# Transforms copied out of PSUM once, folds and sums from SBUF, and a new list order

## The chip, the cores and the metric

The kernel runs on one core of one Trainium2 chip. The metric is device microseconds of one execution, the median over runs. The kernel before took 450.99 us: three runs of 451.47, 450.99 and 449.7.

## The reference, cut to what matters

```python
x = A_x                                        # 2048 x 448, float32
xn = layernorm(x)                              # mean and variance over 448
y = irfft2(rfft2(xn) * (w_r + 1j * w_i))       # over both axes
gate, up = x @ W_gate, x @ W_up                # 448 -> 1792
h = gate * (gate > 0) * up
return x + y + h @ W_down                      # 1792 -> 448
```

Two branches stand side by side: a Fourier filter over the whole of the normalised input, and a gated feed-forward layer. Everything is float32. TensorE is given float16 high and low parts (three products for one) where that is enough.

## The kernel before, in words

**Feed-forward branch.** The 1792 features are 14 tiles of 128, in three groups of 5, 5 and 4. The 2048 tokens are four chunks of 512, taken in the order 0, 2, 1, 3. One feature tile of one chunk is a gate unit, 56 in all: 28 matmuls of 128x512 into one of two PSUM buffers named `gu`. A gate step follows each unit: ScalarE applies the ReLU (L1058), VectorE multiplies by the up half (L1062), ScalarE makes the float16 high part `h` (L1066), VectorE the low part (L1070). When a group's units of one chunk are done, down units (`dn`, 128x448) follow: ScalarE seeds the accumulator (L1087) and takes it out again (L1098). At the very end `dn_end` does the last four token tiles without a seed; its last 12 matmuls (L1126) go into the transforms' buffer.

**Forward transform.** Tokens are split as 16 columns of 128 rows of work; columns a and a+8 are a pair, and the eight pairs are taken in the order 0, 4, 2, 6, 1, 5, 3, 7. For one pair:

- `f_dft`: 48 small matmuls (`fx<-fd_t,T`), the transform along the 448.
- `f_dft` ends with a ScalarE copy of one half of the result (L527); `f_fold` (L539, twice) adds and subtracts the other half, read from PSUM, to give `eb`.
- `f_a` and `f_b`: an eight-point butterfly on `eb` on VectorE (L463 to L468, L473 to L490).
- `f_sdft`: four float32 matmuls (`fx<-eb,fm`, eight rows of the trace) along the tokens.
- `f_y1`: one half copied by ScalarE (L611), then sum and difference with the other half, read from PSUM (L615, L616).

The butterflies across pairs (`stage2` to `stage4`, L590 to L604), the product with the filter and the inverse butterflies follow.

**Inverse transform**, for one pair p: `i_pair` joins two sides, `i_mix` does the eight-point butterfly on `wst` (half 0 is L463 to L468, half 1 is L477 to L490), `i_hi` and `i_lo` make the float16 parts `vt` (L840, L845), `i_sdft` is 48 matmuls (`fx<-im,vt`), `i_part` copies one half of the result (L864), `i_unfold` adds and subtracts the other half from PSUM (L869, twice), `i_pqhi` and `i_pqlo` make the float16 parts `wf` (L875, L879), and `i_ddft` is 48 matmuls (`fx<-idc_t,wf`). `i_ddft` is seeded and taken out by ScalarE (L890, L906), and the rows are stored.

All transforms share one PSUM buffer of two banks, `fx`: a transform can begin only when all readers of the one before it are done. `two_banks` opens it for `f_dft` with a ScalarE write of one element (L507).

**What sets the order.** The opening (loads, layer norm, weights, the first gate units) stands in an order written out by hand (`OPENING`). From there the program issues gate and down units in a fixed sequence, and between them items of one list, `bg`. Each item has a cost in VectorE microseconds:

```python
add(1.27, f_fold, 0)                       # cost, function, arguments
```

Each gate or down unit earns credit, and `run_bg` issues list items while the credit lasts. So the list's order and costs decide behind which TensorE unit a step is issued. Two list entries are special: `offer` lets a transform be placed inside the next unit, between two half-height passes that stand together (`gu_halves`), and `force` places it now if that has not happened. The framework's scheduler then sets each engine's final order by priority; `tc.high_priority` pulls matmuls of a block together and the copies forward. All engines run their own queue in order.

Of the kernel before, what the change touches and what calls it, by code (L numbers as in the profile page):

```python
# [19 lines left out]
KC = 29  # L20
# [142 lines left out]
def tile_gfnet_reglu(ctx: ExitStack, tc: tile.TileContext, x, xr, wgu, wd, wf, ident, c_fd, c_fm, c_im, c_row, c_id,  # L163
# [289 lines left out]
        copy(Tq[q][:, (3, 4, 8)[i], :], tp["end", i], act)  # L453


    fi = {}
    Fq, Xh, yps, cur, fa, fps = {}, {}, {}, {}, {}, {}
    RT = float(np.sqrt(0.5))

    def eight_a(F, w):  # L460
# [48 lines left out]

    def f_dft(a, b, m=None):  # L510

        ps = fps[a] = two_banks()
        T = Tq[a % 4]
        for k, n2 in enumerate((a, b)):
            js = slice(128 * (n2 // 4), 128 * (n2 // 4 + 1))
            for r in range(4):
                o = slice((4 * k + r) * GW, (4 * k + r + 1) * GW)
                for i, (t, part) in enumerate(((r, "h"), (r, "l"), (5 + r, "h"))):
                    c = fd_off[part, r]
                    for h in (1, 0):  # L520
                        p = slice(64 * h, 64 * h + 64)
                        with tc.high_priority(offset=2000):
                            m = chained(mm(ps[:, 1 - h, o], T[p, t, js], fd_t[p, c:c + GW], start=(k + r + i == 0),
                                                 stop=(i == 2), skip_group_check=True).ins, m)
        t = fa[a] = free.pop(0)
        with tc.high_priority(offset=400):
            A.activation(flat(t).rearrange("p (i e) -> p i e", i=2), ps[:, :, 0:4 * GW], AF.Copy,  # L527
                         scale=2.0 ** -14)
        return m

    def f_fold(a):

        k = fi[a] = NG * (len(fi) % 2)
        F = Fq[a] = state["eb"][:, k:k + NG]
        F = F.rearrange("p (i s) c (b k) -> p b i (s c) k", i=2, b=2)
        t = flat(fa[a]).rearrange("p (i x k) -> p i x k", i=2, k=KC)
        ps = fps.pop(a)[:, :, 4 * GW:8 * GW].rearrange("p i (x k) -> p i x k", k=KC)
        for b in range(2):
            V.scalar_tensor_tensor(F[:, b], ps, (-1.0) ** b * 2.0 ** -14, t, op0=OP.mult, op1=OP.add)  # L539
        free.append(fa.pop(a))  # L540

    def f_a(a):
        eight_a(Fq[a], state["eb"][:, 2 * NG:])
# [14 lines left out]

    def f_sdft(a):
        m, w, ps = None, fm_t[a], fx2()  # L560
        for k in range(2):
            yps[a + 8 * k] = ps[:, k, 0:XW].rearrange("p (c g k) -> p c g k", g=NG, c=2)
        for k in range(2):
            for b in range(2):
                p, q = slice(64 * k, 64 * k + 64), slice(64 * b, 64 * b + 64)
# [39 lines left out]
        free.extend(st)  # L605
        return sb, sa

    def f_y1(n2):
        if n2 < 8:
            t = free.pop(0)  # L610
            A.activation(t, yps[n2], AF.Copy)  # L611
            cur["y", n2] = t
        else:
            a, ps, t = cur.pop(("y", n2 - 8)), yps[n2], free.pop(0)
            V.tensor_tensor(t, a, ps, op=OP.add)  # L615
            V.tensor_tensor(a, a, ps, op=OP.subtract)  # L616
            cur["s1", n2 - 8, 0], cur["s1", n2 - 8, 1] = t, a

    def level(far, k, p, ks, sgn, src, dst, *js):

# [239 lines left out]
        return m  # L860

    def i_part(p):
        yu[p] = it([128, 2, 512], F32, "yu", 1)
        A.activation(yu[p][:, 1], sps[p][:, 0], AF.Copy, scale=2.0 ** -14)  # L864

    def i_unfold(p):
        y, ps = yu[p], sps.pop(p)
        for b in range(2):
            V.scalar_tensor_tensor(y[:, b], ps[:, 1], (-1.0) ** b * 2.0 ** -14, y[:, 1], op0=OP.mult, op1=OP.add)  # L869

    def i_pqhi(p):
        t = it([128, 2, 1024], F16, "wf", 3).rearrange("p x (h k) -> p x h k", h=2)
# [305 lines left out]
    seq = [0, 4, 2, 6, 1, 5, 3, 7]  # L1178
    extra = {1: [(ln_chunk, 1)], 2: [(rows_in, 3)], 3: [(ln_chunk, 3)], 4: [(join2, 0, 2)]}
    add(0.0, f_dft, 0, 8)  # L1180
    add(1.27, f_fold, 0)
    for k, a in enumerate(seq):
        gap = k and extra.get(k - 1)
        for second in (False, True):
            if second:
                add(1.99, f_a, a)
            if k and second != bool(gap):
                for n2 in (seq[k - 1], seq[k - 1] + 8):
                    add(1.09 * (n2 >= 8), f_y1, n2)
            if k < 7 and second != bool(gap):  # L1190
                add(0.0, offer, f_dft, seq[k + 1], seq[k + 1] + 8)
        add(2.14, f_b, a)
        if k < 7:
            add(0.0, force, f_dft, seq[k + 1], seq[k + 1] + 8)
            add(1.27, f_fold, seq[k + 1])
        add(0.0, f_sdft, a)
        for fn, *qs in extra.get(k, ()):
            fn(*qs)
    for n2 in (7, 15):
        add(1.09 * (n2 >= 8), f_y1, n2)  # L1200
    join2(1, 3)
    join3()
    add(0.0, open_inv)
# [55 lines left out]
    bring(0)  # L1259
    bring(1)  # L1260
    add(0.0, load_im, 0)
    add(1.1, i_pair, 0)
    add(1.99, i_mix, 0, 0)
    for p in range(8):
        if p:
            add(1.2, i_pqlo, p - 1)
            add(0.0, offer, i_ddft, p - 1, p + 7)
        if p < 7:
            add(0.0, load_im, p + 1)
        add(2.14, i_mix, p, 1)  # L1270
        add(0.0, i_hi, p)
        if p < 6:
            bring(p + 2)
        add(1.1, i_lo, p)
        if p:
            add(0.0, force, i_ddft, p - 1, p + 7)
        add(0.0, i_sdft, p)
        add(0.0, i_part, p)
        if p < 7:
            add(1.1, i_pair, p + 1)  # L1280
        add(1.3, i_unfold, p)
        add(0.0, i_pqhi, p)
        if p < 7:
            add(1.99, i_mix, p + 1, 0)
    add(1.2, i_pqlo, 7)
    add(0.0, i_ddft, 7, 15)

# [291 lines left out]
```

## Time and profile before

| what | value |
|---|---|
| median of three runs | 450.99 us |
| profiled execution | 450.99 us, of which the span is 449.2 us |
| busy TensorE (PE) / its weight loads (PEld) | 430.8 us / 202.5 us |
| busy VectorE (DVE) / ScalarE (ACT) / GpSimd (POOL) | 376.9 / 247.3 / 29.0 us |
| mean granted TensorE clock | 0.988 |
| DMA | 38.63 MB, 86 GB/s on average |

The span runs from the first instruction to the last; the execution's own time is 1.8 us longer. Busy times are sums over an engine's instructions, so a wait shows as the difference between a stretch's length and an engine's busy time in it. Each row of a group names the source line, the engine, the operation and the tiles (`out<-in`), then busy microseconds, the mean nanoseconds of one, the idle time just before them on that engine and the instruction that ended most of it. A timeline row has its start, its length, and in brackets an idle time before it and its releaser.

### The profile page before, as it was taken

The numbers are of one execution on the slowest core, as the hardware profiler recorded it, in microseconds if no ns is written. First come the engines' busy times: TensorE is split into PE (matmuls) and PEld (weight loads), VectorE is DVE, ScalarE is ACT, GpSimd is POOL, SyncE is SP. The second block draws the span as 40 slices with busy tenths as digits, with TensorE's granted clock in tenths as the row PEclk, the third lists the DMA queues.
The fourth block names the chain that finished last, engine by engine and source line by source line (L and its number), as shares of the span: only waits on it lengthen the run. The fifth ranks groups of instructions, "written<-read, shape, count | busy, mean of one in ns | idle before, by whom it ended". The sixth has DMA issues, their size and how long they took to land.

```text
span 449.2 us, 8454 instructions
## 1 busy us (share of the span) xinstructions
PE 430.8 (96%) x3222; PEld 202.5 (45%) x3222; DVE 376.9 (84%) x808; ACT 247.3 (55%) x500; POOL 29.0 (6%) x72
## 2 busy tenths in 40 slices
PE   6999999999999999989999999999999994999997
PEld 2644544444454344434444444444544542444544
DVE  6898796969956979999999999899999899758513
ACT  6897282746356727626333733663776664563630
POOL 1140040300000010000000021010000000000000
PEclk9999999999999999999999999999999996999999
DMA  7769937140002171136413100031022302200212
GB/s 256 247 167 296 376 129 108 29 81 0 1 2 91 61 227 50 39 89 170 116 54 95 34 0 2 0 85 44 8 51 50 84 8 77 79 22 1 83 43 82
DMA packets 37721, 38.63 MB, mean 86 GB/s; under 512 B 18928, under 2 KB 33072, under 8 KB 37680
## 3 DMA queue, kind: packets, MB, share of 16 engines
q1 hardware_dynamic: 37680, 38.09, 29.9%
q8 instruction: 25, 0.41, 0.4%
q14 instruction: 16, 0.13, 0.1%
HBM read 23.20 MB, written 3.67 MB: 60 GB/s over the span
## 4 chain that ended last, share of the span: by engine, by line
PE 53%; DVE 30%; DMA 5%; SPq 5%; ACT 4%; issue 2%; DVEq 0%; ACTq 0%
PE gu L499 30%; PE dn L499 16%; PE fx L499 5%; SPq L723 4%; DVE g L1062 3%; DMA sw<-y 2%; DVE h L1070 2%; DVE y L591 2%; DVE y L590 2%; DVE wt L958 1%; DVE y L603 1%; DVE y L731 1%; PE dn L1126 1%; ACT junk L234 1%; DVE y L689 1%
## 5 line engine op out<-in xcount | busy, mean ns | idle before, releaser
L499 PE MATMUL gu<-T,wt 128*128 128x512 f16 (+2 forms) x1250 | 270.5, 379 | 1.7 <-DVE g L1062 1.6
L499 PEld LDWEIGHTS <-wt 128*128 128x128 f16 (+1 forms) x1250 | 112.2, 98 | 147.7 <-issue 28.2
L499 PE MATMUL dn<-wdt,h 128*128 128x448 f16 x624 | 127.4, 353 | 1.1 <-ACT dn L1087 0.6
L499 PEld LDWEIGHTS <-h 128*128 128x128 f16 x624 | 59.6, 98 | 61.0 <-issue 3.6
L1066 ACT ACTIVATE h<-g 128x512 f16<-128x512 f32 x56 | 35.1, 627 | 83.0 <-DVE g L1062 82.8
L1062 DVE SCALAR_TENSOR_TENSOR g<-gu,g 128x512 f32<-128x512 f32 x56 | 38.3, 684 | 19.2 <-ACT g L1058 19.1
L1070 DVE TENSOR_TENSOR h<-g,h 128x512 f16<-128x512 f32 x56 | 38.6, 690 | 8.4 <-ACT h L1066 8.4
L1058 ACT ACTIVATE g<-gu 128x512 f32<-128x512 f32 x56 | 32.8, 586 | 13.4 <-PE gu L499 13.2
L1098 ACT ACTIVATE xy<-dn,dsc 128x448 f32<-128x448 f32 x44 | 27.4, 626 | 20.1 <-PE dn L499 20.1
L1087 ACT ACTIVATE dn<-xy,dinv 128x448 f32<-128x448 f32 x44 | 27.5, 629 | 0.5
L237 POOL PARTITION_ALL_REDUCE wm<-wm x15 | 9.1, 608 | 187.8 <-ACT junk L234 187.8
L958 DVE SCALAR_TENSOR_TENSOR wt<-wst,wsc,wt 128x512 f16<-128x512 f32 x28 | 20.3, 745 | 0.3 <-ACT wt L954 0.3
L539 DVE SCALAR_TENSOR_TENSOR eb<-fx,y 128x464 f32<-128x464 f32 x16 | 9.5, 634 | 13.1 <-ACT y L527 13.1
L954 ACT ACTIVATE wt<-wst,wsc 128x512 f16<-128x512 f32 x28 | 19.1, 713 | 1.8 <-DVE wsc L244 1.8
L234 ACT ACTIVATE junk<-wst 128x512 bf16<-128x512 f32 x28 | 17.4, 622 | 2.8 <-DMA wst<-in_wgu 2.5
L681 ACT ACTIVATE wf<-wf 128x116 f32<-128x116 f32 x16 | 4.5, 296 | 19.6 <-DMA wf<-in_wf 11.6
L840 ACT ACTIVATE vt<-wst,fsc 128x928 f16<-128x928 f32 x8 | 8.8, 1100 | 9.7 <-DVE wst L490 9.7
L591 DVE TENSOR_TENSOR y<-y 128x928 f32<-128x928 f32 (+1 forms) x11 | 11.8, 1074 | 2.6 <-DMA row<-y 2.6
L499 PE MATMUL fx<-idc_t,wf 64*128 64x56 f16 x384 | 7.9, 189 | 6.2 <-DVE wst L467 4.9
L307 DVE BATCH_NORM_STATS2 bst<-y 128x6 f32<-128x448 f32 x16 | 9.2, 617 | 5.2 <-DMA y<-in_xr 5.2
L869 DVE SCALAR_TENSOR_TENSOR yu<-fx,yu 128x512 f32<-128x512 f32 x16 | 11.0, 688 | 2.7 <-ACT yu L864 2.4
L845 DVE SCALAR_TENSOR_TENSOR vt<-wst,fsc,vt 128x464 f16<-128x464 f32 x16 | 10.5, 698 | 2.3 <-ACT vt L840 2.3
(156 smaller groups left out, 466.4 us busy)
## 6 DMA issues: line engine op xcount, KB each, us to landing
wst<-in_wgu SPq DMA_DIRECT2D x28, 256.0 KB, 4.5
wf<-in_wf SPq DMA_DIRECT2D x16, 232.0 KB, 3.2
sw<-y SPq DMA_DIRECT2D x64, 58.0 KB, 2.0
sw<-wst SPq DMA_DIRECT2D x32, 116.0 KB, 2.2
y<-in_xr SPq DMA_DIRECT2D x16, 224.0 KB, 4.8
xy<-in_x SPq DMA_DIRECT2D x16, 224.0 KB, 4.9
out<-xy SPq DMA_DIRECT2D x15, 224.0 KB, 1.9
wdst<-in_wd SPq DMA_DIRECT2D x14, 224.0 KB, 4.5
```

The source lines that it names most:

```text
L234: A.activation(mt([128, 512], BF16, "junk")[:, 0:src.shape[-1]], src, AF.Square, scale=SQ, accum_out=acc)
L499: r = P.matmul(*a, **k)
L591: V.tensor_tensor(b, a, b, op=OP.subtract)
L723: nc.sync.dma_start(t[o, n], cur[key][i])
L954: A.activation(w[:, 0:4, :], wst[f, g], AF.Copy, scale=wsc[f, g])
L958: V.scalar_tensor_tensor(w[:, 4:8, :], st, sc, w[:, 0:4, :], op0=OP.mult, op1=OP.subtract)
L1058: last["A"] = A.activation(g1s[f, q], hps[f, q][:, 0, :], AF.Relu, scale=2.0 ** -22).ins
L1062: last["V"] = V.scalar_tensor_tensor(g1, hps[f, q][:, 1, :], 2.0 ** -22, g1, op0=OP.mult, op1=OP.mult).ins
L1066: A.activation(ht[f, q][:, 0, :], g1s[f, q], AF.Copy)
L1070: V.tensor_tensor(h[:, 1, :], g1s.pop((f, q)), h[:, 0, :], op=OP.subtract)
L1087: A.activation(dps[n2][:, 0:D], xy[n2], AF.Copy, scale=dinv[:, g:g + 1])
L1098: last["A"] = A.activation(xy[n2], dps[n2][:, 0:D], AF.Copy, scale=dsc[:, g:g + 1]).ins
```

## The change

Three things are changed.

1. *Copies.* `f_dft` copies the whole result (928 elements a partition, two `y` buffers) by one ScalarE copy. A new `f_y`, right behind `f_sdft`, copies both its halves (928) by one ScalarE copy. `i_part` copies both halves of `i_sdft`'s result (1024) into a `wf` buffer.
2. *VectorE.* `f_fold`, `f_y1` and `i_unfold` read only SBUF, by plain additions and subtractions.
3. *List order and costs.* Forward: the fold of the next pair stands behind `f_sdft` and `f_y` of this pair and behind the extra work; the sums of the pair before stand between `f_a` and `f_b`; `offer` stands ahead of `f_a`. Inverse: `i_pair` and `i_mix` half 0 of the next pair stand ahead of `i_unfold`; half 1 and `i_hi` stand behind `i_pqhi`.

```diff
--- before.py
+++ after.py
@@ -453,8 +453,8 @@
         copy(Tq[q][:, (3, 4, 8)[i], :], tp["end", i], act)
 
 
-    fi = {}
-    Fq, Xh, yps, cur, fa, fps = {}, {}, {}, {}, {}, {}
+    fi, sfx = {}, {}
+    Fq, Xh, yps, cur, fa = {}, {}, {}, {}, {}
     RT = float(np.sqrt(0.5))
 
     def eight_a(F, w):
@@ -509,7 +509,7 @@
 
     def f_dft(a, b, m=None):
 
-        ps = fps[a] = two_banks()
+        ps = two_banks()
         T = Tq[a % 4]
         for k, n2 in enumerate((a, b)):
             js = slice(128 * (n2 // 4), 128 * (n2 // 4 + 1))
@@ -522,10 +522,10 @@
                         with tc.high_priority(offset=2000):
                             m = chained(mm(ps[:, 1 - h, o], T[p, t, js], fd_t[p, c:c + GW], start=(k + r + i == 0),
                                                  stop=(i == 2), skip_group_check=True).ins, m)
-        t = fa[a] = free.pop(0)
+        ts = fa[a] = [free.pop(0) for _ in range(2)]
         with tc.high_priority(offset=400):
-            A.activation(flat(t).rearrange("p (i e) -> p i e", i=2), ps[:, :, 0:4 * GW], AF.Copy,
-                         scale=2.0 ** -14)
+            A.activation(joint(ts).rearrange("p n c g k -> p n (c g k)").rearrange("p n (i e) -> p n i e", i=2),
+                         ps[:, :, 0:8 * GW].rearrange("p i (n e) -> p n i e", n=2), AF.Copy, scale=2.0 ** -14)
         return m
 
     def f_fold(a):
@@ -533,11 +533,11 @@
         k = fi[a] = NG * (len(fi) % 2)
         F = Fq[a] = state["eb"][:, k:k + NG]
         F = F.rearrange("p (i s) c (b k) -> p b i (s c) k", i=2, b=2)
-        t = flat(fa[a]).rearrange("p (i x k) -> p i x k", i=2, k=KC)
-        ps = fps.pop(a)[:, :, 4 * GW:8 * GW].rearrange("p i (x k) -> p i x k", k=KC)
-        for b in range(2):
-            V.scalar_tensor_tensor(F[:, b], ps, (-1.0) ** b * 2.0 ** -14, t, op0=OP.mult, op1=OP.add)
-        free.append(fa.pop(a))
+        ts = fa.pop(a)
+        x, y = (flat(t).rearrange("p (i x k) -> p i x k", i=2, k=KC) for t in ts)
+        V.tensor_tensor(F[:, 0], x, y, op=OP.add)
+        V.tensor_tensor(F[:, 1], x, y, op=OP.subtract)
+        free.extend(ts)
 
     def f_a(a):
         eight_a(Fq[a], state["eb"][:, 2 * NG:])
@@ -558,8 +558,7 @@
 
     def f_sdft(a):
         m, w, ps = None, fm_t[a], fx2()
-        for k in range(2):
-            yps[a + 8 * k] = ps[:, k, 0:XW].rearrange("p (c g k) -> p c g k", g=NG, c=2)
+        sfx[a] = ps
         for k in range(2):
             for b in range(2):
                 p, q = slice(64 * k, 64 * k + 64), slice(64 * b, 64 * b + 64)
@@ -605,16 +604,18 @@
         free.extend(st)
         return sb, sa
 
-    def f_y1(n2):
-        if n2 < 8:
-            t = free.pop(0)
-            A.activation(t, yps[n2], AF.Copy)
-            cur["y", n2] = t
-        else:
-            a, ps, t = cur.pop(("y", n2 - 8)), yps[n2], free.pop(0)
-            V.tensor_tensor(t, a, ps, op=OP.add)
-            V.tensor_tensor(a, a, ps, op=OP.subtract)
-            cur["s1", n2 - 8, 0], cur["s1", n2 - 8, 1] = t, a
+    def f_y(a):
+        yps[a] = [free.pop(0) for _ in range(2)]
+        with tc.high_priority(offset=400):
+            A.activation(joint(yps[a]).rearrange("p n c g k -> p n (c g k)"), sfx.pop(a)[:, :, 0:XW], AF.Copy)
+
+    def f_y1(a):
+        x, y = yps.pop(a)
+        t = free.pop(0)
+        V.tensor_tensor(t, x, y, op=OP.add)
+        V.tensor_tensor(x, x, y, op=OP.subtract)
+        free.append(y)
+        cur["s1", a, 0], cur["s1", a, 1] = t, x
 
     def level(far, k, p, ks, sgn, src, dst, *js):
 
@@ -860,13 +861,15 @@
         return m
 
     def i_part(p):
-        yu[p] = it([128, 2, 512], F32, "yu", 1)
-        A.activation(yu[p][:, 1], sps[p][:, 0], AF.Copy, scale=2.0 ** -14)
+        t = state["eo"] = it([128, 2, 1024], F16, "wf", 3).bitcast(F32)
+        with tc.high_priority(offset=400):
+            A.activation(t, sps.pop(p), AF.Copy, scale=2.0 ** -14)
 
     def i_unfold(p):
-        y, ps = yu[p], sps.pop(p)
-        for b in range(2):
-            V.scalar_tensor_tensor(y[:, b], ps[:, 1], (-1.0) ** b * 2.0 ** -14, y[:, 1], op0=OP.mult, op1=OP.add)
+        t = state["eo"]
+        y = yu[p] = it([128, 2, 512], F32, "yu", 1)
+        V.tensor_tensor(y[:, 0], t[:, 0], t[:, 1], op=OP.add)
+        V.tensor_tensor(y[:, 1], t[:, 0], t[:, 1], op=OP.subtract)
 
     def i_pqhi(p):
         t = it([128, 2, 1024], F16, "wf", 3).rearrange("p x (h k) -> p x h k", h=2)
@@ -1178,26 +1181,23 @@
     seq = [0, 4, 2, 6, 1, 5, 3, 7]
     extra = {1: [(ln_chunk, 1)], 2: [(rows_in, 3)], 3: [(ln_chunk, 3)], 4: [(join2, 0, 2)]}
     add(0.0, f_dft, 0, 8)
-    add(1.27, f_fold, 0)
+    add(1.15, f_fold, 0)
     for k, a in enumerate(seq):
-        gap = k and extra.get(k - 1)
-        for second in (False, True):
-            if second:
-                add(1.99, f_a, a)
-            if k and second != bool(gap):
-                for n2 in (seq[k - 1], seq[k - 1] + 8):
-                    add(1.09 * (n2 >= 8), f_y1, n2)
-            if k < 7 and second != bool(gap):
-                add(0.0, offer, f_dft, seq[k + 1], seq[k + 1] + 8)
-        add(2.14, f_b, a)
+        if k < 7:
+            add(0.0, offer, f_dft, seq[k + 1], seq[k + 1] + 8)
+        add(2.1, f_a, a)
+        if k:
+            add(1.15, f_y1, seq[k - 1])
+        add(2.2, f_b, a)
         if k < 7:
             add(0.0, force, f_dft, seq[k + 1], seq[k + 1] + 8)
-            add(1.27, f_fold, seq[k + 1])
         add(0.0, f_sdft, a)
+        add(0.0, f_y, a)
         for fn, *qs in extra.get(k, ()):
             fn(*qs)
-    for n2 in (7, 15):
-        add(1.09 * (n2 >= 8), f_y1, n2)
+        if k < 7:
+            add(1.15, f_fold, seq[k + 1])
+    add(1.15, f_y1, 7)
     join2(1, 3)
     join3()
     add(0.0, open_inv)
@@ -1259,29 +1259,30 @@
     bring(0)
     bring(1)
     add(0.0, load_im, 0)
-    add(1.1, i_pair, 0)
-    add(1.99, i_mix, 0, 0)
+    add(1.4, i_pair, 0)
+    add(2.1, i_mix, 0, 0)
+    add(2.5, i_mix, 0, 1)
+    add(0.0, i_hi, 0)
     for p in range(8):
         if p:
             add(1.2, i_pqlo, p - 1)
             add(0.0, offer, i_ddft, p - 1, p + 7)
-        if p < 7:
-            add(0.0, load_im, p + 1)
-        add(2.14, i_mix, p, 1)
-        add(0.0, i_hi, p)
         if p < 6:
             bring(p + 2)
-        add(1.1, i_lo, p)
+        add(1.3, i_lo, p)
         if p:
             add(0.0, force, i_ddft, p - 1, p + 7)
         add(0.0, i_sdft, p)
         add(0.0, i_part, p)
         if p < 7:
-            add(1.1, i_pair, p + 1)
-        add(1.3, i_unfold, p)
+            add(0.0, load_im, p + 1)
+            add(1.4, i_pair, p + 1)
+            add(2.1, i_mix, p + 1, 0)
+        add(1.2, i_unfold, p)
         add(0.0, i_pqhi, p)
         if p < 7:
-            add(1.99, i_mix, p + 1, 0)
+            add(2.5, i_mix, p + 1, 1)
+            add(0.0, i_hi, p + 1)
     add(1.2, i_pqlo, 7)
     add(0.0, i_ddft, 7, 15)
 
```

How the order on TensorE moves is shown at three places. Names are tiles with their numbers; `fx`, `gu` and `dn` are PSUM buffers, what stands behind the arrow are the operands.

The first place is TensorE's queue at pair 4 of the inverse transform, around 370 us; before, the last rows of the block `fx<-im,vt` and the first of `fx<-idc_t,wf`:

```order
L499 MATMUL fx_4363<-im_4013,vt_2107 128x64
L499 LDWEIGHTS vt_2107
L499 MATMUL fx_4363<-im_4013,vt_2107 128x64
L499 LDWEIGHTS wf_4418
L499 MATMUL fx_4539<-idc_t_67,wf_4418 128x56
```

After, behind the same block:

```order
L499 LDWEIGHTS vt_2057
L499 MATMUL fx_4351<-im_4178,vt_2057 128x64
L499 LDWEIGHTS h_4231
L499 MATMUL dn_4710<-wdt_3607,h_4231 128x448
L499 LDWEIGHTS h_4231
L499 MATMUL dn_4710<-wdt_3607,h_4231 128x448
L499 LDWEIGHTS h_4479
L499 MATMUL dn_4710<-wdt_3981,h_4479 128x448
```

The second block of pair 4 has moved back: 25 down and 17 gate matmuls now stand between the two, then four matmuls of the block, four down matmuls and the block's other 44.

The second place is TensorE's queue at the second transform of forward pair 2, in the part around 80 us. Before, with down matmuls in the midst of it and gate matmuls behind:

```order
L499 LDWEIGHTS h_1171
L499 MATMUL dn_1347<-wdt_569,h_1171 128x448
L499 MATMUL fx_1144<-eb_83,fm_999 64x464 x4
L499 LDWEIGHTS h_1171
L499 MATMUL dn_1347<-wdt_569,h_1171 128x448
L499 LDWEIGHTS wt_397
L499 MATMUL gu_1508<-T1_64,wt_397 128x512
```

After, the same block:

```order
L499 LDWEIGHTS wt_242
L499 MATMUL gu_1174<-T1_64,wt_242 128x512
L499 LDWEIGHTS wt_197
L499 MATMUL gu_1174<-T1_64,wt_197 128x512
L499 MATMUL fx_1111<-eb_83,fm_1009 64x464 x4
L499 LDWEIGHTS T1_64
L499 MATMUL fx_1200<-fd_t_82,T1_64 128x58
```

The first transform of pair 1 (`fx<-fd_t,T1`) now follows the block with nothing between; before, matmuls of gate and down units stood there.

The third place is the end of TensorE's queue. Before, the last down matmuls into a `gu` buffer, then the 12 into `fx`:

```order
L1126 LDWEIGHTS h_5295
L1126 MATMUL gu_5301<-wdt_3868,h_5295 128x224
L1126 LDWEIGHTS h_5295
L1126 MATMUL gu_5301<-wdt_3868,h_5295 128x224
L1126 LDWEIGHTS h_5147
L1126 MATMUL fx_5302<-wdt_3585,h_5147 128x224
```

After, ahead of the same 12:

```order
L499 MATMUL fx_5040<-idc_t_67,wf_5037 128x56
L499 LDWEIGHTS wf_5037
L499 MATMUL fx_5040<-idc_t_67,wf_5037 128x56
L1129 LDWEIGHTS h_5154
L1129 MATMUL fx_5309<-wdt_3604,h_5154 128x224
```

The last inverse transform has moved back, past the other down matmuls of `dn_end`, and stands just ahead of the last 12.

## The prediction

> **What bounds the kernel now.** I read the page's busy shares first, then the same busy times cut into stretches, then TensorE's own waits, and last the one stretch in which TensorE stands still. Columns of the second view: length of the stretch, then busy microseconds (and instructions) of each engine, granted clock, DMA.
>
> ```profile
> PE 430.8 (96%) x3222; PEld 202.5 (45%) x3222; DVE 376.9 (84%) x808; ACT 247.3 (55%) x500; POOL 29.0 (6%) x72
> ```
> ```profile
> 40.00:140.00 100.00, 100.00 (x821) 45.67 (x820) 78.75 (x185) 54.69 (x116) 11.09 (x28) 1.00 0.38 103
> 180.00:320.00 140.00, 137.13 (x714) 62.06 (x714) 135.15 (x243) 68.29 (x150) 5.42 (x6) 1.00 0.23 59
> 368.00:384.00 16.00, 8.80 (x153) 4.66 (x145) 15.86 (x38) 7.77 (x12) 0.00 (x0) 0.68 0.25 68
> 384.00:420.00 36.00, 36.00 (x398) 17.78 (x396) 25.54 (x55) 18.68 (x30) 0.00 (x0) 1.00 0.13 39
> 420.00:446.00 26.00, 25.90 (x187) 13.60 (x185) 8.02 (x13) 9.16 (x15) 0.00 (x0) 1.00 0.17 63
> ```
>
> TensorE (PE) is the bound: it never stops from 40 to 140 us and again after 384, and the change takes none of its matmuls away. So the time can move only through TensorE's gaps. There are two behind the opening: 2.9 us in all between 180 and 320 (140.00 less 137.13), where VectorE (DVE) is busy for 135 of 140 us, and 7.2 us between 368 and 384, where the clock also falls to 0.68 on average. Who is waited for:
>
> ```profile
> PE fx L499 <- DVE wst L467: 4.9, 1, 4.9
> PE fx L499 <- DVE wf L879: 1.3, 1, 1.3
> PE gu L499 <- DVE g L1062: 1.6, 2, 1.3
> PE fx L499 <- ACT xy L906: 0.9, 1, 0.9
> ```
>
> Three of these four are one place. TensorE's rows there, then what it waits for, then its clock:
>
> ```profile
> 368.33 0.59 PE L499 MATMUL gu<-T,wt 64*128 64x512 f16 x4
> 369.81 1.30 PE L499 MATMUL fx<-im,vt 64*128 64x64 f16 x48 [0.88 <-ACT xy L906]
> 376.02 0.28 PE L499 MATMUL fx<-idc_t,wf 64*128 64x56 f16 x4 [4.91 <-DVE wst L467]
> 377.61 1.21 PE L499 MATMUL fx<-idc_t,wf 64*128 64x56 f16 x44 [1.32 <-DVE wf L879]
> 378.75 5.51 PE L499 MATMUL gu<-T,wt 128*128 128x512 f16 x14
> ```
> ```profile
> 371.15 0.60 ACT L864 ACTIVATE yu<-fx 128x512 f32<-128x512 f32 x1 [0.91 <-PE fx L499]
> 372.33 1.41 DVE L869 SCALAR_TENSOR_TENSOR yu<-fx,yu 128x512 f32<-128x512 f32 x2
> 374.40 1.04 ACT L875 ACTIVATE wf<-yu 128x1024 f16<-128x1024 f32 x1
> 376.34 1.22 DVE L879 TENSOR_TENSOR wf<-yu,wf 128x1024 f16<-128x1024 f32 x1
> ```
> ```profile
> 373.30:383.20 9.90, 5.86 (x59) 2.94 (x60) 9.80 (x26) 4.29 (x6) 0.00 (x0) 0.50 0.24 73
> ```
>
> In TensorE's queue the second inverse transform of pair 4 (`fx<-idc_t,wf`) stands right behind its first one (`fx<-im,vt`), with nothing between. So TensorE lies open to the whole chain that turns the one's output into the other's input: copy (L864), unfold (L869), high half (L875), low half (L879). At other pairs gate or down matmuls stand between and the chain is hidden. The price: an undisturbed pair of blocks takes 0.87 and 0.79 us,
>
> ```profile
> 419.08 0.87 PE L499 MATMUL fx<-im,vt 64*128 64x64 f16 x48
> 429.23 0.79 PE L499 MATMUL fx<-idc_t,wf 64*128 64x56 f16 x48
> 430.12 1.16 ACT L906 ACTIVATE xy<-fx,fsc 128x448 f32<-128x448 f32 x2 [3.10 <-PE fx L499]
> ```
>
> so the next gate matmul could start at 368.92 + 0.87 + 0.79 = 370.6 and starts at 378.75: 8.2 us. The half clock then holds until about 383.4, 4.65 us of work at half speed, 2.3 us more. Together 10.5 us.
>
> **The change, part by part.** *VectorE from SBUF instead of PSUM.* Forms, with mean ns of one:
>
> ```profile
> L539 DVE SCALAR_TENSOR_TENSOR eb<-fx,y 128x464 f32<-128x464 f32 x16 | 9.5, 634 | 13.1 <-ACT y L527 13.1
> L463 DVE TENSOR_TENSOR eb<-eb 128x464 f32<-128x464 f32 x8 | 5.1, 640 | 0.2
> L615 DVE TENSOR_TENSOR y<-y,fx 128x464 f32<-128x464 f32 x8 | 5.0, 630 | 0.1
> L869 DVE SCALAR_TENSOR_TENSOR yu<-fx,yu 128x512 f32<-128x512 f32 x16 | 11.0, 688 | 2.7 <-ACT yu L864 2.4
> L1070 DVE TENSOR_TENSOR h<-g,h 128x512 f16<-128x512 f32 x56 | 38.6, 690 | 8.4 <-ACT h L1066 8.4
> L922 DVE SCALAR_TENSOR_TENSOR xy<-fx,fsc,xy 128x224 f32<-128x224 f32 x4 | 1.5, 444 | 0.0
> L527 ACT ACTIVATE y<-fx 128x464 f32<-128x464 f32 x8 | 4.4, 546 | 6.8 <-PE fx L499 6.8
> L875 ACT ACTIVATE wf<-yu 128x1024 f16<-128x1024 f32 x8 | 8.3, 1043 | 1.6 <-DVE yu L869 1.6
> ```
>
> Forty-eight instructions change their source: 16 folds, 16 sums, 16 unfolds. A fold from PSUM takes 634 ns, an SBUF add of the same width (L463) 640; an unfold 688 against 690 for L1070. So VectorE saves nothing on them, between -0.1 and +0.1 us in all. [...] Apart from that, four L922 of the one pair that the scheduler treats differently go (1.8 us of VectorE, late, where it has slack: nothing).
>
> *ScalarE.* Eight copies each of 928, 928 and 1024 elements in place of 464, 464 and 512. One of 1024 (L875) takes 1043 ns; twice a 464 copy would be 1.09. I take 0.95, 0.95 and 1.02: some 0.4 us more for each, 10 us in all on an engine that is 55% busy. Hidden by gate and down matmuls, except where a transform stands bare (below).
>
> *Order, inverse side.* In the new queue every pair has matmuls between its two blocks. For pair 4 they are 25 down and 17 gate matmuls, four of the block itself, and four more down: by
>
> ```profile
> 321.10 5.02 PE dn L499 x26
> 327.79 7.77 PE gu L499 x36
> ```
>
> 0.193 and 0.216 us each, 29 x 0.193 + 17 x 0.216 = 9.3 us (the other seven have 7.4 to 11.2). To hide: copy 1.02, unfold 1.41, low half 1.22, and now also the second half of the mixing step, which the new list puts between unfold and low half:
>
> ```profile
> 363.86 0.27 DVE L477 TENSOR_TENSOR wst<-wst 128x116 f32<-128x116 f32 x1
> 367.10 0.40 DVE L490 SCALAR_TENSOR_TENSOR wst<-wst 128x232 f32<-128x232 f32 x1
> ```
>
> these are its first and last rows, 3.6 us with two gate steps of 0.6 among them, so 2.4 alone. Sum 6.1 us, 7.4 with one pair of gate steps in between: covered by 9.3. VectorE's work ahead of the gate step of pair 4 is the same as before, and after it the new queue asks for each result later than the old, so it isn't late there. The stall goes: **-10.5 us**. What is late next is nothing in this stretch: from 384 on VectorE is busy for 25.54 of 36 us.
>
> *Order, forward side.* The second transform of pair 2 (`fx<-eb,fm`) and the first of pair 1 (`fx<-fd_t,T`) now stand back to back. Both use the single `fx` buffer, so TensorE waits for the copy of the first:
>
> ```profile
> 77.52 1.02 PE L499 MATMUL fx<-eb,fm 64*64 64x464 f32 x8
> 78.79 0.54 ACT L611 ACTIVATE y<-fx 128x464 f32<-128x464 f32 x1
> ```
>
> 0.25 us from the block's end (78.54) to the copy's start, 0.95 for the wider copy, 0.2 for the small write that opens the next block: **+1.4 us**. Bounds: 1.1 if the copy takes 0.6, 2.6 if ScalarE is two 0.6 us instructions behind.
>
> *Order, middle.* By the 17th gate step on VectorE the new list has done 10.4 us more: the last fold and eight-point step, four sums (0.6 each, 2.4) and three stage-2 instructions (2.6). The step's first row and the row behind its last:
>
> ```profile
> 145.02 1.18 DVE L539 SCALAR_TENSOR_TENSOR eb<-fx,y 128x464 f32<-128x464 f32 x2
> 153.12 0.63 DVE L615 TENSOR_TENSOR y<-y,fx 128x464 f32<-128x464 f32 x1
> ```
>
> 8.1 us apart with 2.7 of gate steps and weight halves between, so 5.4. VectorE is idle for 21.2 us between 40 and 140 (100.00 less 78.75), 13.1 of it at the folds that waited for a transform's copy, and just ahead of that gate step it idled again:
>
> ```profile
> 142.06 0.69 DVE L1062 SCALAR_TENSOR_TENSOR g<-gu,g 128x512 f32<-128x512 f32 x1 [3.49 <-ACT g L1058]
> ```
>
> In the new list each transform is issued before a full eight-point step of the pair ahead, so the folds find their copy done; 10.4 us fit into 21.2 + 3.5. VectorE then enters 180 to 320 with less left to do and TensorE's 2.9 us there shrink. Ends: 0 and 2.9; I take **-2.0**, nearer the second because the work left before gate step 38 is equal in both orders.
>
> *Order, end.* The last inverse transform was followed by nine down matmuls and more; now only the last 12 matmuls of the kernel follow, into the same `fx` buffer. They wait for the two evacuating copies (430.12 to 431.28, while the block's last matmul ended at 430.02): **+1.3 us**, 0 to 4 if the chain for the last pair is itself late: it has 8.2 us less 0.8 of its own block, against 5.0 of chain and a final add of 0.7 that VectorE now does in between.
>
> Sum: 449.2 - 10.5 - 2.0 + 1.4 + 1.3 = 439.4 us of span; the profiled execution took 450.99, 1.8 us more than its span and equal to the median of the three runs, so the time is **441.2 us**.
>
> **Rivals.** *The work moved forward isn't absorbed (ends slower).* If the folds still wait for their transforms, up to 10.4 us of VectorE work stands ahead of gate steps 17 to 36, and TensorE, which has two gate buffers, waits for them: 439.4 + 10.4 + 2.0 + 2.8 (half clock once a wait is long, as above) + 1.8 = 456. For: VectorE is at 97% between 180 and 320. Against: the 24.7 us of idle before. It decides when more than 9 us of the 10.4 stay. [...]
>
> *The stall moves.* Cover and chain at one other pair part by 9 us less than I count, because VectorE gets there late: one such place gives the 10.5 us back, 451.7, no change. For: pairs 0 and 1 have 1 us of margin if VectorE keeps its old lag. Against: a lag of 1 us costs 1 us, not 10; only back-to-back blocks cost it all.
>
> *The bare transforms cost more.* ScalarE late at the forward pair (2.6) and the last pair late (4) give 441.2 + 1.2 + 2.7 = 445; with nothing gained in the middle 447.
>
> *It doesn't do what it says.* VectorE is no faster from SBUF, by the rows above; only the order matters. That is my forecast already, and without the order's effect the time would be 451.
>
> **Numbers.** Forecast 0.70 (437.5 to 444), bare transforms dearer 0.14 (444 to 448), stall moved or no effect 0.09 (about 451), not absorbed 0.07 (453 to 456). Range 437.5 to 447.5, its low end with the middle gap and half of the two bare waits gone. 0.5% is 2.3 us, about what a measurement of this kernel tells from no change: faster 0.84, same 0.09, slower 0.07.
>
> **What would show it.** Right: no TensorE wait above 2 us past 40 us, the clock at 1.00 from there to the last matmul; a wait of 1 to 2 us for ScalarE at the bare forward pair near 84 us and another ahead of the last 12 matmuls; VectorE idle before the folds far below 13.1 us; folds and unfolds at 630 to 690 ns. Wrong: TensorE waits for VectorE's gate steps between 140 and 300 us, or for a low half between 310 and 430 with the clock at 0.50.

## The result and the profile after

The changed kernel takes 445.0 us (median of four runs, 443.72 to 445.91) against 450.43 before: a ratio of 0.9876, 95% interval 0.9841 to 0.9911. It is faster, by 5.4 us; the forecast was 9.8 (450.99 to 441.2). The profiled execution took 444.57 us, its span is 442.8. All numbers of traces below are of single profiled executions.

The same two views as before: busy time of each engine, then the stretches (length, busy time and instructions of PE, PEld, DVE, ACT, POOL, granted clock, DMA).

```profile
PE 429.2 (97%) x3222; PEld 201.6 (46%) x3222; DVE 376.6 (85%) x804; ACT 261.1 (59%) x503; POOL 29.5 (7%) x72
```
```profile
40.00:140.00 100.00, 96.51 (x843) 44.56 (x842) 84.02 (x198) 56.87 (x107) 12.08 (x27) 0.98 0.38 99
180.00:320.00 140.00, 139.47 (x731) 63.72 (x730) 131.51 (x241) 73.56 (x157) 4.08 (x6) 1.00 0.23 60
368.00:384.00 16.00, 16.00 (x169) 7.91 (x168) 14.35 (x34) 10.33 (x16) 0.00 (x0) 1.00 0.20 51
```

The stall at 368 to 384 us is gone: TensorE is busy for 16.00 of 16 us, at full clock, where it was 8.80 at 0.68. The middle lost 2.3 us of gaps (139.47 against 137.13). But from 40 to 140 us, where TensorE had no gap, 3.5 us are now missing, and the clock dips to 0.98 on average. What TensorE waits for past the opening:

```profile
PE fx L499 <- ACT fx L507: 3.5, 1, 3.5
PE fx L1129 <- ACT xy L909: 1.3, 1, 1.3
PE gu L499 <- DVE g L1065: 0.5, 1, 0.5
```

The first row is the bare forward pair, the second the last 12 matmuls. At the forward pair, TensorE's rows and then ScalarE's:

```profile
82.60 1.02 PE L499 MATMUL fx<-eb,fm 64*64 64x464 f32 x8
87.11 1.34 PE L499 MATMUL fx<-fd_t,T 64*128 64x58 f16 x48 [3.49 <-ACT fx L507]
```
```profile
82.98 1.23 ACT L388 ACTIVATE y<-y,rs 128x448 f32<-128x448 f32 x2 [1.11 <-DVE eb L539]
84.11 1.21 ACT L390 ACTIVATE tt<-y,rs 128x448 f16<-128x448 f32 x2
85.23 0.57 ACT L1061 ACTIVATE g<-gu 128x512 f32<-128x512 f32 x1
85.77 0.26 ACT L405 ACTIVATE tt<-tt 128x64 f16<-128x64 f16 x1
85.93 0.92 ACT L610 ACTIVATE y<-fx 128x928 f32<-128x928 f32 x1
86.89 0.17 ACT L507 ACTIVATE fx<-eps 128x1 f32<-128x1 f32 x1
```

The block of pair 2 ended at 83.6, but its copy (L610) starts at 85.93: four layer-norm instructions (L388, L390), a ReLU and a small copy stand ahead of it in ScalarE's queue. The first of them is done as the block ends; the other five take the 2.3 us. The clock after the wait, in one row of stretches:

```profile
86.60:90.00 3.40, 2.89 (x52) 1.78 (x52) 3.40 (x9) 2.21 (x5) 0.53 (x2) 0.50 0.62 118
```

2.89 us of work at half clock cost 1.45 us more. The parts add up: 449.2 - 10.5 (stall and its half clock) - 2.3 (middle) + 3.5 + 1.45 (forward pair) + 1.3 (end) = 442.65, against a span of 442.8.

The forms whose source went from PSUM to SBUF, and the wider copies (duration in ns: least, median, most):

```profile
L538 DVE TENSOR_TENSOR eb<-y x8: 629/642/668, 50.7 to 132.0; 128x464 f32<-128x464 f32 x8
L871 DVE TENSOR_TENSOR yu<-wf x8: 685/692/693, 315.2 to 430.7; 128x512 f32<-128x512 f32 x8
L610 ACT ACTIVATE y<-fx x8: 922/926/945, 62.5 to 143.2; 128x928 f32<-128x928 f32 x8
```

A fold's addition takes 642 ns (its subtraction, L539, 655) where a fold step took 634, an unfold 692 where it took 688: nothing gained by reading SBUF.

### The profile page after: what moved, and what is told of

It reads as the page before. It is cut to its first block, busy times and chain, and to the rows that moved or that the text cites. A ratio compares the mean times of both kernels' runs of the same rounds, so it can differ in the third digit from the quotient of the medians.

```text
span 442.8 us, 8438 instructions
## 1 busy us (share of the span) xinstructions
PE 429.2 (97%) x3222; PEld 201.6 (46%) x3222; DVE 376.6 (85%) x804; ACT 261.1 (59%) x503; POOL 29.5 (7%) x72
## 4 chain that ended last, share of the span: by engine, by line
PE 49%; DVE 31%; DMA 8%; ACT 4%; SPq 3%; issue 3%; POOL 1%; ACTq 0%; DVEq 0%; POOLq 0%
PE gu L499 27%; PE dn L499 15%; PE fx L499 5%; DMA wst<-in_wgu 3%; DMA y<-in_xr 3%; DVE g L1065 2%; SPq L724 2%; DVE h L1073 2%; DVE y L589 2%; DVE y L590 2%; DVE y L690 2%; DVE y L691 2%; DMA sw<-y 2%; DVE y L603 1%; DVE y L602 1%
## 5 line engine op out<-in xcount | busy, mean ns | idle before, releaser
L1069 ACT ACTIVATE h<-g 128x512 f16<-128x512 f32 x56 | 35.1, 627 | 57.5 <-DVE g L1065 57.4
L237 POOL PARTITION_ALL_REDUCE wm<-wm x15 | 7.7, 515 | 174.9 <-ACT junk L234 174.9
L909 ACT ACTIVATE xy<-fx,fsc 128x448 f32<-128x448 f32 x16 | 9.3, 631 | 15.3 <-PE fx L499 15.3
L871 DVE TENSOR_TENSOR yu<-wf 128x512 f32<-128x512 f32 x8 | 5.5, 691 | 9.1 <-ACT wf L866 9.1
L590 DVE TENSOR_TENSOR y<-y 128x928 f32<-128x928 f32 (+1 forms) x11 | 11.8, 1077 | 0.3 <-DMA row<-y 0.2
L589 DVE TENSOR_TENSOR y<-y 128x928 f32<-128x928 f32 (+1 forms) x11 | 11.9, 1077 | 0.2
L866 ACT ACTIVATE wf<-fx 128x1024 f32<-128x1024 f32 x8 | 8.1, 1018 | 5.9 <-PE fx L499 5.9
L846 DVE SCALAR_TENSOR_TENSOR vt<-wst,fsc,vt 128x464 f16<-128x464 f32 x16 | 10.5, 697 | 0.5 <-ACT vt L841 0.4
L473 DVE TENSOR_TENSOR wst<-wst 128x116 f32<-128x116 f32 x48 | 10.5, 273 | 0.2
```

Of the source, the lines that this page charges most:

```text
L589: V.tensor_tensor(t, a, b, op=OP.add)
L590: V.tensor_tensor(b, a, b, op=OP.subtract)
L1069: A.activation(ht[f, q][:, 0, :], g1s[f, q], AF.Copy)
```

## The experiments

Eleven kernels ran. The theory: one badly placed transform (pair 4, inverse) was the loss before, and another badly placed one (pair 1, forward) is the loss now; copies and SBUF reads have little to do with either. The rivals give the gain to the copies or to VectorE, or hold that a stall only moves.

**E1, the placement alone.** Before, with one number changed.

```diff
-        state["job"] = (state["at"], fn, a, 6.0)
+        state["job"] = (state["at"], fn, a, 10.0 if fn is i_ddft else 6.0)
```

> The kernel before with one number changed: an inverse second transform is placed inside a gate unit only when 10.0 us of units, not 6.0, have passed since it was offered. No copy, no VectorE instruction and nothing of the forward side changes; from pair 4 on the second transform stands one gate unit later, with 24 gate and 23 down matmuls between pair 4's two blocks. Theory (the gain of the change is one stall, and the stall is one placement): the wait of 4.9 and 1.3 us at pair 4 and the half clock behind it go, 10.5 us, and 450.4 becomes 440 (438.5 to 442), below the changed kernel's 445.0; VectorE's forms keep their durations and its 2.9 us of TensorE gaps between 180 and 320 us stay. Rival (VectorE's reads of PSUM or the list's order make the chain late, and one placement only moves the stall to a neighbour): 447 to 452, with a new TensorE wait above 3 us at another inverse pair.

Measured: 440.24 us, ratio 0.9766 (0.9752 to 0.9781). Its stretches:

```profile
180.00:320.00 140.00, 137.36 (x718) 62.24 (x716) 135.18 (x243) 68.54 (x150) 5.42 (x6) 1.00 0.23 59
368.00:384.00 16.00, 16.00 (x191) 7.94 (x182) 14.26 (x34) 10.05 (x17) 0.00 (x0) 1.00 0.20 51
```

The stall goes, the middle gap (2.64 us) stays, nothing moves to a neighbour. One number is worth 10.2 us, almost twice the whole change, with every PSUM read in place.

**E2, the copies alone.** The changed kernel's functions under the old list and costs.

```diff
-        for n2 in (seq[k - 1], seq[k - 1] + 8):
-            add(1.09 * (n2 >= 8), f_y1, n2)
+        add(0.0, f_y, seq[k - 1])
+        add(1.09, f_y1, seq[k - 1])
...
(the rest of both lists as before)
```

> The changed kernel's copies and SBUF reads under the list order and costs of before (each f_y stands where the first of the two f_y1 stood). In TensorE's queue pair 4's two inverse blocks are back to back as before, and no forward blocks are. Theory (only the order matters): the stall at pair 4 stays, 0.4 us longer by the wider copy, with its half clock; the middle gaps may shrink a little: 450.5 (448 to 452.5). Rival (reading SBUF in place of PSUM spares VectorE work and the early copies free the shared buffer, which is the gain): 445 or less, with the middle gap of 2.9 us closed and folds and unfolds measurably shorter than 634 and 688 ns.

Measured: 450.89 us, ratio 1.0007 (0.9995 to 1.0019): no change. TensorE at pair 4, and the middle stretch:

```profile
369.58 1.63 PE L499 MATMUL fx<-im,vt 64*128 64x64 f16 x48 [1.72 <-ACT xy L909]
375.16 0.27 PE L499 MATMUL fx<-idc_t,wf 64*128 64x56 f16 x4 [3.95 <-ACT wf L878]
377.37 1.21 PE L499 MATMUL fx<-idc_t,wf 64*128 64x56 f16 x44 [1.93 <-DVE wf L882]
```
```profile
180.00:320.00 140.00, 139.31 (x775) 63.67 (x773) 133.86 (x246) 72.36 (x155) 3.99 (x6) 1.00 0.22 58
```

The stall is there with all its parts, and a little longer (7.6 us of waits against 7.1). The middle gap has closed to 0.7 us under the old order all the same. But TensorE has a new wait, at 95 us, ahead of the middle:

```profile
PE dn L499 <- ACT dn L1090: 1.6, 1, 1.6
```

It is a down unit's, for the seed that ScalarE writes. It holds TensorE for 1.6 us, in which VectorE catches up, so this run doesn't show how much of the closing is due to the copies. TensorE's gaps from 40 to 320 us (length less busy time) add up to 2.3 us, 0.6 less than before, and the longer stall takes 0.5 of it back.

**E3, the bare forward pair.** The changed kernel with one item moved, at one pair.

```diff
-        if k < 7:
+        if k < 7 and k != 3:
             add(0.0, offer, f_dft, seq[k + 1], seq[k + 1] + 8)
         add(2.1, f_a, a)
+        if k == 3:
+            add(0.0, offer, f_dft, seq[k + 1], seq[k + 1] + 8)
```

> The changed kernel with one list item moved: the forward transform of pair 1 is offered behind f_a of pair 6, not ahead of it. Gate and down matmuls then stand behind the second transform of pair 2 (13 and 14 of them). Theory (the 3.5 us wait there and 2.9 us of work at half clock, which cost 1.45, are what the prediction under-priced): 445.0 - 4.9 = 440.1 (439 to 442), no TensorE wait above 1.5 us past 40 us except the last one, clock 1.00. Rival (VectorE is the bound on the forward side, so the wait turns up at the next fold or gate step): 443.5 to 446, with TensorE waits for VectorE between 90 and 180 us.

Measured: 441.02 us, ratio 0.9785 (0.977 to 0.98), 4.0 us below the changed kernel.

```profile
40.00:140.00 100.00, 100.00 (x867) 45.92 (x866) 85.03 (x200) 60.43 (x117) 13.33 (x28) 1.00 0.39 100
140.00:180.00 40.00, 40.00 (x199) 17.18 (x197) 36.26 (x72) 25.93 (x61) 2.49 (x10) 1.00 0.42 129
180.00:320.00 140.00, 138.46 (x750) 62.92 (x750) 133.59 (x246) 71.40 (x149) 3.29 (x6) 1.00 0.22 57
```

No gap from 40 to 180 us, so the wait did not turn up behind it. One us of the 4.9 came back in the middle (1.54 us of gaps where the changed kernel has 0.53): with TensorE no longer held at 84 us, VectorE is later by comparison. The changed kernel's 0.53 us thus owe something to its own wait of 3.5 us.

**E4 and E5, the end.** The last 12 matmuls go into the free half of a gate buffer, in the changed kernel (E4) and in E3's (E5).

```diff
-        banks += [psum.tile([128, 2, 512], F32, name="gu", bufs=2)[:, 0] for _ in range(2)]
-        banks.append(fx())
+        gu2 = [psum.tile([128, 2, 512], F32, name="gu", bufs=2) for _ in range(2)]
+        banks += [gu2[0][:, 0], gu2[1][:, 0], gu2[0][:, 1]]
```

> The changed kernel, but the last 12 matmuls go into the second half of a gate buffer instead of the transforms' buffer. Theory: their wait of 1.31 us for the two evacuating copies goes and the end comes 1.3 us sooner: 443.7 (443 to 444.5). Rival (the end is set by the last transform's copies, the final add and the store, whatever the matmuls do): 445.0, same as the changed kernel within 0.4 us.

Measured: E4 445.02 us, no change, though the wait of 1.3 us is gone from its trace. The reason lies elsewhere. Its wait at the forward pair was as long (3.51 us), but the half clock behind it lasted twice as long:

```profile
86.20:93.00 6.80, 5.92 (x59) 2.83 (x59) 6.80 (x16) 4.18 (x8) 2.21 (x6) 0.51 0.47 87
```

The row's clock is 0.51 because its first 0.2 us ran at full speed: the half clock lasted from 86.38 to 93.20, with 6.1 us of work that cost 3.1 us more, against 1.45 in the changed kernel's profile. From the end of the last transform to the end of the last add E4 takes 2.3 us, the changed kernel 3.1. The two spans agree with that: 442.8 + 1.6 - 0.8 = 443.6, which is E4's. The spread (the changed kernel's four runs lie 2.2 us apart, E1's four 0.3) hides an effect of this size in the medians, so the edit was repeated on E3.

> The two edits together: the forward transform of pair 1 offered behind f_a of pair 6, and the last 12 matmuls in the second half of a gate buffer. Without the wait at pair 1 the half clock and its spread are gone, so that the end can be read. Theory: from the end of the last inverse transform to the end of the last add the own bank alone took 2.3 us where the changed kernel took 3.1; 441.0 - 0.8 = 440.2 (439.6 to 440.6). Rival (the end does not hang on those matmuls): 441.0 within 0.3.

Measured: E5 440.54 us (439.43 to 440.61), against E3's 441.02 (440.58 to 441.57). From the end of the last transform to the end of the last add, E3 and then E5:

```profile
432.62 0.74 PE L499 MATMUL fx<-idc_t,wf 64*128 64x56 f16 x44
436.02 0.45 DVE L1108 SCALAR_TENSOR_TENSOR xy<-fx,dsc,xy 128x224 f32<-128x224 f32 x1 [0.68 <-PE fx L1129]
```
```profile
432.71 0.74 PE L499 MATMUL fx<-idc_t,wf 64*128 64x56 f16 x44
435.34 0.44 DVE L1108 SCALAR_TENSOR_TENSOR xy<-gu,dsc,xy 128x224 f32<-128x224 f32 x1
```

433.36 to 436.47 is 3.1 us, 433.45 to 435.78 is 2.3: 0.8 us in the traces, 0.5 between the medians, whose ranges touch. The wait of 1.1 us was worth less than itself, since the adds wait for the same two copies (L909) in any case: VectorE is idle for 2.0 us until the first of them in both traces.

**E6, the layer norm in place.** It lets the normalising step start without waiting for a buffer that the fold frees.

```diff
-        xn_b[n2] = free.pop(0)
+        xn_b[n2] = xr_b.pop(n2)
...
-        free.append(xr_b.pop(n2))
```

> The changed kernel, with the layer norm's first ScalarE step written in place instead of into a buffer of the pool, for the two chunks done inside the list. The two blocks of forward pairs 2 and 1 stay back to back on TensorE; what goes is the wait of the normalising step (1.11 us) for the buffer that the fold of pair 2 gives back, so the four layer-norm instructions no longer stand between the block and its copy. Theory (the wait of 3.5 us was ScalarE's queue, not the copy): it falls to the predicted 1.4 us (1.1 to 2.2), too short for the half clock, and 445.0 becomes 441.5 (440.5 to 442.5). Rival (the wider copy and the shared buffer alone make the wait): above 3 us still and 444 to 446.

Measured: 446.75 us (444.56 to 447.65), not faster. TensorE's rows (line numbers are one lower here):

```profile
84.09 1.01 PE L498 MATMUL fx<-eb,fm 64*64 64x464 f32 x8 [1.44 <-ACT y L526]
87.38 1.34 PE L498 MATMUL fx<-fd_t,T 64*128 64x58 f16 x48 [2.27 <-ACT fx L506]
```

The expectation failed. The layer norm ran earlier, and so stood in front of the copy one transform earlier: 1.4 and 2.3 us in place of one 3.5, and 6.8 us of half clock behind them (86.56 to 93.38). That a wait of 1.4 us is too short for the half clock was the author's estimate; in the kernel before, one of 1.3 us, between 180 and 320 us, passed at a clock of 1.00, and in E2 one of 1.7 us did not. So it is not one buffer: what stands in ScalarE's queue around 78 to 87 us decides.

**E7, copies and later offer.** E2 with E1's number.

> The new copies and SBUF reads under the old list order, with the later offer (10.0 us) of the inverse second transforms. Theory (the placement is worth 10.5 us under either way of reading): 450.9 - 10.5 = 440.4 (439 to 441.5), the clock at 1.00 past 40 us; against the later offer alone (440.24) the copies bring nothing but the closing of the middle gap, 2 us, less their 1.6 us wait of a down matmul for ScalarE. Rival (the copies' wider ScalarE work costs on TensorE): 442 to 444.

Measured: 439.94 us (439.48 to 440.88), ratio 0.9767 (0.9744 to 0.9789), 10.95 us below E2. The placement is worth the same under either way of reading. Against E1 (440.24) there is no difference to be measured: the middle gap shrinks from 2.64 to 0.18 us, and a wait of 1.8 us for a seed, ahead of it, takes its place. TensorE's gaps from 40 to 320 us are 1.9 us in all, against 2.6.

```profile
PE dn L499 <- ACT dn L1090: 1.8, 1, 1.8
```

**E8, the forward half alone.** Forward functions and list as changed, the inverse side as before.

> The change's forward half alone: f_dft, f_fold, f_y, f_y1 and the forward list as changed; i_part, i_unfold and the inverse list as before. Pair 4's inverse blocks are back to back again, and so are the forward blocks of pairs 2 and 1, with two layer-norm instructions ahead of the copy instead of four. Theory (the gain is all on the inverse side, the forward side costs): 450.4 - 2.0 (middle) + 2.4 (wait for two layer-norm instructions, copy and opening write) + 0 to 1.7 (one stretch of half clock) = 451 to 453. Rival (the forward part is neutral or gains): 448 to 450.

Measured: 454.44 us, ratio 1.0093 (1.0066 to 1.0119): slower. It has both bare pairs:

```profile
PE fx L499 <- DVE wst L467: 4.7, 1, 4.7
PE fx L499 <- ACT fx L507: 4.1, 1, 4.1
PE fx L499 <- ACT xy L907: 1.6, 1, 1.6
PE fx L499 <- DVE wf L880: 1.3, 1, 1.3
PE fx L499 <- ACT y L527: 1.1, 1, 1.1
```

L507 and L527 are the forward pair (5.2 us), the others pair 4. There is no gap at all from 180 to 320 us, behind this long hold. The half clock behind the forward pair lasted 6.8 us (88.44 to 95.27), where the 1.7 us of the theory is half of one stretch of 3.4, the changed kernel's. The loss is above the expected range; the sign is as the theory has it.

**E9 and E10, layer norm on GpSimd.** Its second step leaves ScalarE, in the changed kernel (E9) and in E7 (E10).

```diff
-        A.activation(tt[n2].rearrange("p a b -> p (a b)")[:, 0:D], xn[n2], AF.Copy, scale=r)
+        G.tensor_scalar(tt[n2].rearrange("p a b -> p (a b)")[:, 0:D], xn[n2], r, None, op0=OP.mult)
```

> The changed kernel, with the second of the two layer-norm steps of the chunks done inside the list (scale to float16) on GpSimd in place of ScalarE. Pairs 2 and 1 stay back to back on TensorE; ScalarE loses the two 0.6 us scaling steps that stood between the block and its copy. With the layer norm in place the wait had only split (1.4 and 2.3 us), which speaks for ScalarE's whole load around 78 to 87 us and not for one buffer. Theory (ScalarE's load there): the wait falls from 3.5 to 1.8 us and with it the half clock, 445.0 - 1.7 - 1.7 = 441.6 (440.5 to 442.8). Rival (the next thing in line, VectorE's fold and gate step or a slower GpSimd step, sets the transform's start anyway): a TensorE wait above 3 us stays or comes back elsewhere before 100 us, 444 to 447.

> The copies under the old list order with the later offer, and the same layer-norm step on GpSimd. In its trace without that step the one TensorE wait above 1 us past 40 us was a down matmul's for its seed, 1.8 us, behind ScalarE's layer norm and copies. Theory: with 0.6 us less on ScalarE for each token tile the wait shrinks, 439.9 becomes 438.5 (437.8 to 439.5). Rival (the wait was VectorE's lag, through ScalarE's queue: ScalarE sat idle 2.8 us for the gate product just ahead of it): 439.9 within 0.5.

Measured: E9 446.68 us, E10 443.68. Both are slower than without the edit (445.0, 439.94), against both theories; E9's rival (444 to 447) came true, E10's (439.9 within 0.5) did not. In E9 the block of pair 2 ends at 84.68, and its copy starts 1.35 us later, where it was 2.3, with the two scaling steps no longer in between. But the small opening write now stands behind another instruction. TensorE's block, then ScalarE, then GpSimd:

```profile
83.66 1.02 PE L499 MATMUL fx<-eb,fm 64*64 64x464 f32 x8
```
```profile
86.03 0.93 ACT L610 ACTIVATE y<-fx 128x928 f32<-128x928 f32 x1
87.97 0.63 ACT L1069 ACTIVATE h<-g 128x512 f16<-128x512 f32 x1 [1.01 <-DVE g L1065]
88.50 0.16 ACT L507 ACTIVATE fx<-eps 128x1 f32<-128x1 f32 x1
```
```profile
82.08 1.83 POOL L390 TENSOR_SCALAR tt<-y,rs 128x448 f16<-128x448 f32 x1 [13.12 <-ACT h L1069]
```

TensorE waits 4.0 us: the copy is done at 86.96, but L507 comes behind the high part `h` (L1069), which waits for VectorE's gate product. The step takes 1.83 us on GpSimd here (1.4 to 2.1 over its eight) against 0.66 on ScalarE. In E10 the wait for the seed grew from 1.8 to 3.5 us and brought 6.8 us of half clock. What of that is GpSimd's slowness and what the new order on ScalarE was not separated.

**E11, the inverse order alone.** Before, with the changed inverse list and its costs, and nothing else.

> The kernel before with the change's inverse list order and costs alone; every copy and every PSUM read as before. All inverse pairs have matmuls between their blocks. But the list's costs are one budget: on the forward side, whose list is untouched, three transforms (pair 6's first, pair 2's second, pair 1's first by their place) now stand with nothing between them on TensorE. Theory: the 10.5 us of pair 4 go without any copy; on the forward side the second transform waits for the copy and two folds from PSUM and the third for a copy and the sums, 4 to 6 us with one or two stretches of half clock, 1.7 each: 445 to 449, with no TensorE wait above 2 us past 300 us. Rival (the inverse order needs the early copies, since unfolds from PSUM hold the buffer): a wait above 3 us past 300 us, and 450 or more.

Measured: 450.28 us, ratio 0.9995 (0.998 to 1.0011), above the expected range. TensorE's waits, and the stretch behind the first:

```profile
PE fx L499 <- ACT fx L507: 4.8, 2, 4.3
PE fx L499 <- ACT h L1066: 4.6, 1, 4.6
```
```profile
85.00:98.40 13.40, 6.37 (x64) 2.79 (x65) 10.91 (x25) 3.40 (x10) 2.53 (x9) 0.50 0.58 90
```

Past 300 us there is no wait of a transform: the inverse order does without the copies, and the rival's 450 came about without its wait there. All of the gain was given back at forward pairs that the edit did not touch: 4.6 and 4.3 us of waits, and 6.7 us of work at half clock from 85.06 to 98.71 (3.3 us; the row above leaves out the last 0.3 us). The list's costs are one budget, so other inverse costs changed where the forward transforms are issued. Both new lists together under the old copies were not run.

## Why the prediction was right, and where it was off

- *The stall, -10.5.* Right, and by the mechanism named. E1 takes it away by the placement alone (-10.2), E7 against E2 again (-10.95), and E2, with all copies and the old order, keeps it.
- *VectorE from SBUF, nothing.* Right: 642 against 634 ns, 692 against 688; E2 gains no time.
- *The wider copies.* Right: 926 and 1018 ns were estimated as 950 and 1020, and in the changed kernel they are hidden except at the bare places. Under the old order (E2, E7) a down unit waits 1.6 to 1.8 us for ScalarE.
- *The middle, -2.0.* The size came out (-2.3), partly by luck. "In the new list each transform is issued before a full eight-point step of the pair ahead, so the folds find their copy done" is what the trace shows: VectorE's idle time before the folds is 2.0 us, against 13.1. But the sum took the middle and the forward pair as independent, and they are not: while TensorE is held, VectorE catches up. In E3, with no hold, VectorE idles 4.9 us before the folds and TensorE's gaps are 1.54 us, so that 1.3 us (2.87 less 1.54) of the 2.3 are left. In E8, held for 5.2 us, there is no gap, though VectorE idles 8.3 us at the folds. How the 1.3 us divide between copies and order was not isolated: E2 and E7 have the copies without the order, but hold TensorE 1.6 and 1.8 us, and their gaps from 40 to 320 us are only 0.6 and 0.7 us shorter in all.
- *The bare forward pair, +1.4.* The place and the engine were right, the size was not: 3.5 us, with 1.45 to 3.1 of slow work behind it, over the upper bound of 2.6. The sign "no TensorE wait above 2 us past 40 us, the clock at 1.00" failed here. I took the 0.25 us from the block's end to the copy's start out of the kernel before, and allowed two ScalarE instructions ahead of it at most. Six stood in the queue there, four of them layer-norm steps, and five had still to run when the block ended; the half clock was not priced at all in this term. E3 gets 4.0 us back by putting gate and down matmuls there.
- *The end, +1.3.* The wait is 1.31 us as worked out, but taking it away is worth only 0.5 to 0.8 us (E5): the adds wait for the same copies.
- *Of the rivals*, "the bare transforms cost more" is what happened, with a chance of 0.14: 445.0, at the place that it named first, though not at the end that it named second. E3's 441.0 beside the forecast of 441.2 is luck in part: E3 has no wait at that pair, where the forecast had 1.4 us, so the other terms together came out 1.2 us too low. The rival "isn't absorbed" adds 2.8 us of half clock "as above", where the working above it has 2.3; its 456 hardly moves by that. No run shows what puts 453 at the low end of its range; of short waits, those of 1.4 and 2.3 us in E6 brought 6.8 us of half clock, and one of 1.8 us in E7 brought none.

The change gains 5.4 us because its order trades the bare pair 4 (10.5 us) for a cheaper bare pair on the forward side (4.0 to 4.9) and a bare end. E1, E3, E5 and E7 lie between 439.9 and 441.0, all below it; E1 does that with a single number.

## What to carry to other kernels

When a bound engine stands still once, look first at what stands on either side of the wait in its own queue: moving the second block one unit later was worth 10.2 us here, and the rewrite of the chain that fed it alone nothing that could be measured (E2). Price a bare wait by the queue of the engine that releases it as it will stand then, instruction by instruction, and add the half clock behind it (1.45 to 3.1 us here behind a wait of 3.5 us). Where costs and order form one budget, an edit at one end can uncover a transform at the other (E11), so read the whole queue of the bound engine after each edit.

## What the hardware showed

In these traces the half clock lasted one to four times 3.41 us. Read in short stretches, it lasted 3.4 us (after: 86.62 to 90.04; E9), 6.8 (E4: 86.38 to 93.20; E6, E8 and E10 likewise), 10.2 (before: 373.24 to 383.48; E2, and E8 at pair 4) and 13.65 (E11: 85.06 to 98.71). Cut into steps of 3.41 us from the fall on, the last step held 2.9 to 3.4 us of TensorE's work in each of the nine traces, every step ahead of it 0.3 to 2.7: in the changed kernel the only step held 2.93, while in E4 the first, with work from 87.08 to 89.79 (2.7 us), was followed by another. So the same wait of 3.5 us cost 1.45 us of slow work in the execution where work began 0.5 us after the fall (87.11), and 3.1 in the one where it began 0.7 us after it (87.08). The 3.41 us ahead of a fall were not empty: they held 0.4 us of work in the changed kernel, 1.2 before and 1.6 in E2. So the length of a wait alone does not tell these cases apart: one of 1.7 us (E2, 367.9 to 369.6) brought half clock, and one of 1.8 us (E7, clock 1.00 from 40 to 140 us) did not.
